# Fused attention and feed-forward on one core: the opening's order and all scheduling rules chosen anew

## Chip, cores, metric

The kernel runs on one core of a Trainium2 chip. The metric is the time of one execution on the device in microseconds (us), taken as the median of several runs. The profile gives a slightly shorter figure, the span from the first to the last instruction of one profiled execution (before: 703.6 us span, 705.5 us time).

## The reference

2048 tokens of width 640 are normalised. Attention with 32 heads of width 20, which share one key and one value head, and a feed-forward layer with squared ReLU both read the normalised tokens, and everything is summed.

```python
def reference(A_x, A_wq, A_wk, A_wv, A_wo, B_x, B_w1, B_b1, B_w2, B_b2):
    x = A_x                                   # 1 x 2048 x 640
    xn = _layernorm(x, axis=-1)
    # attention: q = xn @ wq (32 heads x 20), k = xn @ wk, v = xn @ wv (one head x 20)
    #   p = softmax(q k^T * 20 ** -0.5);  A = (p v, heads side by side) @ wo
    # feed-forward: h = relu(xn @ w1 + b1) ** 2;  B = h @ w2 + b2
    return x + A + B
```

## The kernel before

All 2048 score tiles (128 keys by 512 queries of one head) are made by TensorE and then need an exponential. ScalarE does most, two or three tiles in one instruction:

```python
return Op(f"ACT{st_['j']}", "ACT", 0.05 + 0.4267 * n, [lambda e: e.activation(
    out=PT[:, s0:s0 + n, :], in_=ps[:, b0:b0 + (n - 1) * db + 1:db, :],
    func=AF.Exp, bias=-EXP_SHIFT, scale=SCALE)], deps)
```

VectorE does the rest in *sets* of four tiles: it turns each score into the bit pattern of an exponential (with TensorE, GpSimd and more passes of VectorE behind it).

The program orders its own instructions while it is built: a list scheduler picks the next instruction of each engine by estimates, under some twenty numbers that may be set anew for each 10 us of the kernel's time, a *stage*:

```python
STG = 10.0
RULES = {3: {'PVA': 2.1, 'PVD': 2.1, 'R3': 1, 'PP': 0.9},
         ...                                   # cut: 49 more stages
         69: {'R3': 0, 'JIT': 1.1}}
PRIO = {'NM15': 2.12, 'NM10': 2.88, 'PW2': 0.96}          # hand-set order of single instructions
NBEF = {'AG4': 10.21, 'NM7': 11.5, 'Qe0_1': 10.11, 'PW12': 25.33}   # not before this time
QEACT = (0, 1, 2, 3)                           # query copies of the opening on ScalarE
ACTST = (2, 5, 6)                              # token tiles whose statistics ScalarE takes
POOLXN = (2, 7, 9, 10, 11, 13, 14, 15)         # token tiles that GpSimd normalises
```

The opening loads 16 token tiles of 128 tokens. Each needs statistics, a normalisation (`XN`), a transpose on TensorE (`T`) and a copy of that (`TE`). Four token tiles make a *key group*: one key product, one copy of it, and then 4 x 4 heads = 16 score tiles of the first query block become possible. Once the attention begins, ScalarE is to have scores without a break.

The softmax here doesn't subtract the row's maximum and nothing guards it: scores larger than these inputs give would overflow.

## Time and profile before

| before | |
|---|---|
| time, median of 3 runs | 705.52 us (704.88 to 706.26) |
| first exponential starts | 15.30 us |
| ScalarE idle between exponentials in the opening | 0.39 us at 28.15, 2.35 us at 32.44 |
| exponentials | 715 instructions, 1480 tiles |
| VectorE score tiles | 568 (142 sets) |
| last exponential ends | 695.14 us |
| from there to the end (tail) | 8.50 us |

The table is read from ScalarE's timeline and the page's groups; the prediction shows those lines of the timeline and the chain. In the page's groups, below, the columns are: line, engine, operation, output and input, count, then busy time and mean ns, then idle time just before and what ended it. These two rows of the kernel before split the score tiles between ScalarE and VectorE:

```profile
L910 ACT ACTIVATE PT<-ps 128x1024 bf16<-128x1024 f32 (+1 forms) x715 | 677.1, 1219 | 3.8 <-PE ps L367 3.8
L1083 DVE TENSOR_SCALAR tmore<-ps 128x512 uint16<-128x512 f32 x568 | 367.4, 683 | 31.7 <-PE ps L367 28.2
```

ScalarE waited only 3.8 us in all for scores, so it is the bound.

### The profile page before, as it was taken

To read this page: it belongs to the slowest core of one execution; us is meant where nothing else is said; L and a number is where in the kernel's file an instruction comes from. 1 tells how busy PE (TensorE), PEld (TensorE's weight loads), DVE (VectorE), ACT (ScalarE), POOL (GpSimd) and SP (SyncE) were. 2 spreads that over 40 slices of the span, in tenths; PEclk is the share of its full clock that TensorE was granted. 3 is DMA by queue.
4 is the path that set the end of the run, shared out by engine and by line. 5 is a ranking of instruction groups with operands and counts; after the bars stand their busy time and mean duration, and the time that the engine had idled before them with its cause. 6 is when DMAs were issued, how large, how long until landed. Compare 5 with 4: busy or idle time off the path is not lost.

```text
span 703.6 us, 22608 instructions
## 1 busy us (share of the span) xinstructions
PE 695.0 (99%) x9780; PEld 216.0 (31%) x9781; DVE 645.9 (92%) x1125; ACT 687.5 (98%) x739; POOL 427.3 (61%) x268
## 2 busy tenths in 40 slices
PE   8999999999999999999999999999999999999997
PEld 4422223233322223332322222323333222233333
DVE  7789999999999998989998998899899999999894
ACT  6899999999999999999999999999999999999995
POOL 4767556567566764666568765766665675644253
PEclk9999999999999999999999999999999999999999
DMA  6325422233337701211101001111112100031201
GB/s 201 98 70 153 115 78 58 81 97 80 84 85 160 162 20 25 55 40 37 52 18 40 23 22 28 29 47 26 46 42 51 36 22 23 20 106 51 55 26 39
DMA packets 42016, 44.00 MB, mean 63 GB/s; under 512 B 15540, under 2 KB 32772, under 8 KB 41788
## 3 DMA queue, kind: packets, MB, share of 16 engines
q1 hardware_dynamic: 39132, 36.93, 19.2%
q0 software_dynamic: 2208, 5.25, 3.9%
q8 instruction: 76, 1.25, 0.7%
q10 hardware_dynamic: 576, 0.38, 0.2%
q14 instruction: 24, 0.20, 0.1%
HBM read 28.03 MB, written 14.91 MB: 61 GB/s over the span
## 4 chain that ended last, share of the span: by engine, by line
ACT 95%; PE 4%; DMA 1%; DVE 0%; SPq 0%; issue 0%; DVEq 0%
ACT PT L910 94%; PE ps L367 3%; DMA x_sb<-in_A_x_dram 1%; PE ps L540 1%; ACT xnT L477 0%; ACT OC L421 0%; DVE out_sb L1164 0%; PE ps L568 0%; SPq L384 0%; ACT OC L422 0%; SPq L391 0%; PE ps L510 0%; PE ps L496 0%; DVEq L227 0%; DVE PT L1164 0%
## 5 line engine op out<-in xcount | busy, mean ns | idle before, releaser
L910 ACT ACTIVATE PT<-ps 128x1024 bf16<-128x1024 f32 (+1 forms) x715 | 677.1, 1219 | 3.8 <-PE ps L367 3.8
L1083 DVE TENSOR_SCALAR tmore<-ps 128x512 uint16<-128x512 f32 x568 | 367.4, 683 | 31.7 <-PE ps L367 28.2
L1101 POOL TENSOR_SCALAR tmore<-tmore 128x2048 uint16<-128x2048 uint16 x109 | 206.4, 1900 | 171.1 <-PE ps L367 62.3
L367 PE MATMUL ps<-qT,kT 20*128 20x512 bf16 x2048 | 281.7, 384 | 1.9 <-ACT PT L910 0.8
L1101 POOL TENSOR_SCALAR x_sb<-tmore 128x2048 uint16<-128x2048 uint16 x100 | 189.3, 1902 | 79.4 <-DVE x_sb L1101 24.2
L367 PEld LDWEIGHTS ps<-qT,kT 20*128 20x128 bf16 x2048 | 71.6, 91 | 280.4 <-ACT PT L910 233.1
L367 PE MATMUL ps<-PT,vx 128*32 128x512 bf16 x1480 | 136.9, 386 | 0.2 <-ACT PT L910 0.2
L1101 DVE TENSOR_SCALAR x_sb<-tmore 128x2048 uint16<-128x2048 uint16 x135 | 96.1, 745 | 0.1
L367 PE MATMUL ps<-x_sb,vxs 128*32 128x512 bf16 x940 | 83.2, 382 | 0.0
L367 PE MATMUL ps<-xnT,w_sb 128*32 128x512 bf16 x960 | 77.2, 384 | 0.1
L367 PE MATMUL ps<-w_sb,big 128*32 128x320 bf16 x1536 | 74.5, 302 | 0.0
L367 PE MATMUL ps<-tmore,vxs 128*32 128x512 bf16 x764 | 69.6, 382 | 0.0
L1101 DVE TENSOR_SCALAR tmore<-tmore 128x2048 uint16<-128x2048 uint16 x82 | 61.5, 770 | 0.1
L367 PE MATMUL ps<-tmore,vx 128*32 128x512 bf16 x568 | 55.7, 382 | 0.0
L367 PEld LDWEIGHTS ps<-PT,vx 128*32 128x32 bf16 x1480 | 34.9, 94 | 62.1 <-issue 53.6
L367 PEld LDWEIGHTS ps<-w_sb,big 128*32 128x32 bf16 x1536 | 32.1, 95 | 29.3 <-issue 22.2
L648 DVE TENSOR_SCALAR hT_tmp<-ps,b1col 128x512 bf16<-128x512 f32 x48 | 35.8, 746 | 3.4 <-PE ps L367 2.7
L367 PE MATMUL ps<-xnT,wq_sb 128*32 128x512 bf16 (+1 forms) x480 | 33.7, 356 | 0.2 <-DVE tmore L1083 0.2
L367 PE MATMUL ps<-wo_c,OC 128*32 128x320 bf16 x608 | 30.9, 301 | 0.0
L367 PEld LDWEIGHTS ps<-x_sb,vxs 128*32 128x32 bf16 x940 | 21.3, 95 | 19.9 <-issue 13.4
L367 PEld LDWEIGHTS ps<-xnT,w_sb 128*32 128x32 bf16 x960 | 17.6, 94 | 26.7 <-issue 22.4
L367 PEld LDWEIGHTS ps<-tmore,vxs 128*32 128x32 bf16 x764 | 18.1, 95 | 16.4 <-issue 11.5
(81 smaller groups left out, 259.4 us busy)
## 6 DMA issues: line engine op xcount, KB each, us to landing
xbd<-b2d SPq DMA_DIRECT2D x16, 320.0 KB, 4.4
xbd<-in_A_x_dram POOLq DMA_DIRECT2D x8, 640.0 KB, 5.8
xr<-xbd SPq DMA_DIRECT2D x32, 160.0 KB, 2.4
w_sb<-in_B_w_dram SPq DMA_DIRECT2D x8, 480.0 KB, 4.4
big<-OR SPq DMA_DIRECT2D x71, 40.0 KB
big<-drs SPq DMA_DIRECT2D x71, 40.0 KB
out_dram<-out_sb SPq DMA_DIRECT2D x15, 160.0 KB, 1.8
qT<-QCr SPq DMA_DIRECT2D x108, 20.0 KB
```

The source lines that it names most:

```text
L367: return lambda e: e.matmul(out_, l, r, start=start, stop=stop, tile_position=tp)
L540: return [(lambda e, dt=dt: e.transpose(out=psbf(bk)[:, dt * 128:(dt + 1) * 128], in_=xn_sb[:, st, dt:D:DT], identity=ident[:])) for dt in ...
L648: o = Op(f"RL{qc}_{f}", "DVE", 0.66, [lambda e: e.tensor_scalar(out=hT_tmp[:, k % 2, :], in0=ps[:, bk, :], scalar1=b1col[:, f:f + 1], scal ...
L910: return Op(f"ACT{st_['j']}", "ACT", 0.05 + 0.4267 * n, [lambda e: e.activation(out=PT[:, s0:s0 + n, :], in_=ps[:, b0:b0 + (n - 1) * db + ...
L1083: d1 = op(f"D1_{n}_{i}", "DVE", 0.60, lambda e: e.tensor_scalar(out=L[:, cs].bitcast(U16), in0=ps[:, bank, :], scalar1=XA, scalar2=XB, op0 ...
L1101: p = op(f"P{j}_{n}", eng, 0.60 if eng == "DVE" else 1.86, lambda e, T=T, j=j, two=two: e.tensor_scalar(out=T.bitcast(U16), in0=L.bitcast( ...
```

## The change

The intent is a quicker opening (ScalarE does fewer query copies and its statistics earlier, some hand-set delays go), a gate that keeps VectorE from taking a score while it is busy, and new rules for every stage. Cut to its core:

```diff
-RULES = {3: {'PVA': 2.1, 'PVD': 2.1, 'R3': 1, 'PP': 0.9},
-         ... (cut: 50 more stages)
+DJIT = 9.0
+RULES = {2: {'DRATE': 1.1, 'DGAP': 1.5, 'JIT': 1.1},
+         ... (cut: 52 more stages; 'DJIT': 0.3 in stages 67 to 69 alone)
-PRIO = {'NM15': 2.12, 'NM10': 2.88, 'PW2': 0.96}
-NBEF = {'AG4': 10.21, 'NM7': 11.5, 'Qe0_1': 10.11, 'PW12': 25.33}
+PRIO = {'XN1': 0.13}
+NBEF = {'S4a': 6.0, 'AG5': 10.23, 'PW1': 4.94}
-QEACT = (0, 1, 2, 3)
+QEACT = (0, 1)
-FFN0 = 0.3
+FFN0 = 0.6
-ACTST = (2, 5, 6)
-POOLXN = (2, 7, 9, 10, 11, 13, 14, 15)
+ACTST = (0, 2, 4)
+POOLXN = (7, 9, 10, 11, 13, 14, 15)
@@ make_dqk: a score tile for VectorE
+            if max(free["DVE"], free["PE"]) + sum(o.dur for o in dve_q if o.frees is not None) > free["PE"] + 0.43 + par("DJIT"):
+                return None
```

More of the change, by code (lines that the diff above doesn't have):

```diff
@@ L80 @@
 KEEP = 1
-RULES = {3: {'PVA': 2.1, 'PVD': 2.1, 'R3': 1, 'PP': 0.9},
-         4: {'PVA': 2.1, 'PVD': 2.1, 'R3': 1, 'PP': 0.9, 'WARM': 0.78},
-         5: {'D1P': 1, 'MPRIO': 0.5, 'PBIAS': 2.5},
-         6: {'D1P': 1, 'MPRIO': 0.5, 'PBIAS': 2.5, 'ND': 1, 'QKP': 0},
-         7: {'DQP': 2.05, 'URG': 2, 'PVD': 2.1, 'BEHIND': -0.3},
-         8: {'WARM': 0.85, 'DQP': 0.95},
-         10: {'ND': 1, 'NOPEN': 3},
-         11: {'ND': 1, 'NOPEN': 3},
-         12: {'EPS': 0.12},
-         13: {'EPS': 0.06, 'EVP': 0.3},
-         15: {'PBIAS': 0},
-         17: {'EPS': 0.06},
-         18: {'EPS': 0.12},
-         19: {'WARM': 0.78, 'PBIAS': 2.5, 'IDLE': 0.3},
-         21: {'PBIAS': 0, 'KEEP': 0},
-         23: {'EPS': 0.12},
-         25: {'R3': 1, 'EVP': 0.3},
-         26: {'R3': 1, 'EVP': 0.3, 'IDLE': 0.3, 'PVD': 2.1},
-         28: {'EPS': 0.12, 'URG': 3},
-         29: {'EPS': 0.12, 'URG': 3, 'KEEP': 3, 'EVP': 1.1, 'ND': 3},
-         31: {'PBIAS': 1, 'D1P': 1, 'PVD': 1.05},
-         32: {'PBIAS': 1, 'D1P': 1, 'PVD': 1.05, 'DGAP': 0.8, 'DQP': 0.95, 'SQP': 2, 'R3': 1},
-         36: {'PP': 0.9, 'BEHIND': -0.1, 'EVP': 0.3, 'PBIAS': 1.5},
-         37: {'URG': 3, 'JIT': 1.0, 'PVD': 1},
-         38: {'SQP': 0.7, 'URG': 3},
-         39: {'PP': 2.5},
-         40: {'PBIAS': 1},
-         41: {'PBIAS': 1, 'DGAP': 1.5, 'SQP': 0.7},
-         42: {'PBIAS': 1, 'DGAP': 1.5, 'SQP': 2, 'NOPEN': 3, 'ND': 2, 'PVD': 1},
-         43: {'PBIAS': 1, 'DGAP': 1.5, 'SQP': 2, 'NOPEN': 3, 'ND': 2, 'PVD': 1, 'R3': 9},
-         44: {'WARM': 0.78, 'KEEP': 3, 'DLAST': 7.5},
-         45: {'DGAP': 0.8, 'KEEP': 1, 'D1P': 3},
-         48: {'PBIAS': 1},
-         49: {'PBIAS': 1, 'R3': 1},
-         50: {'PBIAS': 1, 'R3': 1},
-         53: {'DLAST': 3.5},
-         54: {'DLAST': 3.5, 'EPS': 0, 'EVP': 0.3},
-         55: {'DLAST': 3.5, 'EPS': 0, 'EVP': 0.3, 'ND': 1},
-         56: {'EVP': 2, 'MPRIO': 1.0},
-         57: {'R3': 1, 'ND': 1},
-         58: {'BEHIND': -0.1, 'EPS': 0, 'PP': 4, 'R3': 1},
-         59: {'BEHIND': -0.1, 'EPS': 0, 'PP': 4, 'R3': 1, 'DRATE': 0.95, 'DLAST': 10, 'PVA': 2.1},
-         60: {'EVP': 1.1},
-         61: {'EVP': 1.1, 'SQP': 0.7},
-         62: {'EVP': 1.1, 'SQP': 0.7, 'KEEP': 3, 'R3': 1, 'NOPEN': 2, 'D1P': 3},
-         64: {'PP': 0.9, 'DRATE': 0.8},
-         65: {'R3': 1},
-         66: {'R3': 1},
-         67: {'EPS': 0.12, 'PVA': 1.05},
-         68: {'R3': 0},
-         69: {'R3': 0, 'JIT': 1.1}}
@@ new lines @@
+DJIT = 9.0
+RULES = {2: {'DRATE': 1.1, 'DGAP': 1.5, 'JIT': 1.1},
+         3: {'D1P': 0.5, 'R3': 1, 'IDLE': 0.2},
+         4: {'D1P': 0.5, 'R3': 1, 'IDLE': 0.2, 'JIT': 0.75, 'DGAP': 1.5, 'WARM': 0.72},
+         6: {'PBIAS': 1},
+         7: {'D1P': 3, 'DLAST': 8.5},
+         8: {'D1P': 3, 'DLAST': 3.5, 'DQP': 0.95, 'ND': 1, 'PVD': 0.95},
+         9: {'D1P': 3, 'DLAST': 3.5, 'DQP': 0.95, 'ND': 1, 'PVD': 0.95},
+         10: {'D1P': 3, 'DLAST': 3.5, 'DQP': 0.95, 'ND': 1, 'PVD': 0.95, 'URG': 2, 'PP': 2.5},
+         11: {'DQP': 3, 'PBIAS': 2.5, 'MPRIO': 0.9},
+         12: {'DQP': 3, 'PBIAS': 2.5, 'MPRIO': 0.9, 'PP': 2.5},
+         13: {'DQP': 3, 'PBIAS': 2.5, 'MPRIO': 0.9, 'PP': 2.5},
+         14: {'DQP': 3, 'PBIAS': 2.5, 'MPRIO': 0.9, 'PP': 2.5, 'D1P': 3},
+         15: {'DQP': 3, 'PBIAS': 2.5, 'MPRIO': 1.1, 'PP': 2.5, 'D1P': 3, 'NOPEN': 3},
+         16: {'DQP': 3, 'PBIAS': 2.5, 'MPRIO': 1.1, 'PP': 2.5, 'D1P': 3, 'NOPEN': 3, 'EPS': 0.06},
+         17: {'DQP': 3, 'PBIAS': 2.5, 'MPRIO': 1.1, 'PP': 2.5, 'D1P': 3, 'NOPEN': 3, 'EPS': 0.06},
+         18: {'D1P': 1, 'DRATE': 0.8, 'PBIAS': 1.5},
+         19: {'D1P': 1, 'DRATE': 0.8, 'PBIAS': 1.5},
+         20: {'ND': 2, 'R3': 9, 'EPS': 0.06},
+         24: {'NOPEN': 1},
+         25: {'IDLE': 0.5, 'PBIAS': 2.5},
+         26: {'IDLE': 0.5, 'PBIAS': 2.5, 'SQP': 0.7, 'PP': 2.5},
+         27: {'IDLE': 0.5, 'PBIAS': 2.5, 'SQP': 0.7, 'PP': 2.5, 'URG': 6, 'BEHIND': 0.12},
+         28: {'IDLE': 0.5, 'PBIAS': 2.5, 'SQP': 0.7, 'PP': 2.5, 'URG': 6, 'BEHIND': 0.05, 'NOPEN': 1, 'D1P': 3},
+         29: {'IDLE': 0.5, 'PBIAS': 2.5, 'SQP': 0.7, 'PP': 2.5, 'URG': 6, 'BEHIND': 0.05, 'NOPEN': 1, 'D1P': 3},
+         33: {'DQP': 2.05, 'QKP': 0, 'KEEP': 3},
+         34: {'DQP': 2.05, 'QKP': 0, 'KEEP': 3, 'PP': 0.9},
+         35: {'KEEP': 3},
+         36: {'KEEP': 3, 'DRATE': 1.1, 'DQP': 0.95},
+         37: {'JIT': 0.75, 'MPRIO': 0.9, 'PP': 0.9, 'PVD': 1.05},
+         43: {'DRATE': 0.95, 'WARM': 0.85, 'PBIAS': 1.5},
+         44: {'R3': 0, 'JIT': 0.9, 'DQP': 2.05},
+         45: {'R3': 0, 'JIT': 0.9, 'DQP': 2.05},
+         46: {'DLAST': 3.5, 'D1P': 0.5, 'R3': 1},
+         47: {'DLAST': 3.5, 'D1P': 0.5, 'R3': 1, 'EPS': 0, 'QKP': 0},
+         48: {'DLAST': 3.5, 'D1P': 0.5, 'R3': 1, 'EPS': 0, 'QKP': 0, 'DGAP': 0, 'PP': 0.9},
+         49: {'DLAST': 3.5, 'D1P': 0.5, 'R3': 1, 'EPS': 0, 'QKP': 0, 'DGAP': 0, 'PP': 0.9, 'PBIAS': 0},
+         50: {'PP': 0.9, 'PBIAS': 1.5},
+         51: {'DLAST': 4.5},
+         52: {'PVA': 1, 'PBIAS': 0.3},
+         53: {'PVA': 1, 'PBIAS': 0.3, 'R3': 1, 'IDLE': 2, 'WARM': 0.78},
+         56: {'PBIAS': 1.5, 'DQP': 3, 'DGAP': 0.8, 'JIT': 1.0},
+         57: {'R3': 2, 'URG': 6, 'PP': 2.5},
+         58: {'R3': 2, 'URG': 6, 'PP': 2.5, 'DQP': 0.95, 'IDLE': 2, 'D1P': 0.5},
+         59: {'WARM': 0.78, 'EVP': 2},
+         60: {'PVA': 1, 'R3': 1},
+         61: {'R3': 2, 'KEEP': 3},
+         63: {'DQP': 2.05, 'R3': 1, 'D1P': 0.5, 'NOPEN': 2},
+         64: {'DQP': 2.05, 'R3': 1, 'D1P': 0.5, 'NOPEN': 2, 'URG': 2, 'PVA': 1, 'PBIAS': 0},
+         65: {'DQP': 2.05, 'R3': 1, 'D1P': 0.5, 'NOPEN': 2, 'URG': 2, 'PVA': 1, 'PBIAS': 0},
+         66: {'DQP': 2.05, 'R3': 1, 'D1P': 0.5, 'NOPEN': 2, 'URG': 6, 'PVA': 1, 'PBIAS': 0, 'PP': 0.9, 'DRATE': 0.95},
+         67: {'DQP': 2.05, 'R3': 1, 'D1P': 0.5, 'NOPEN': 2, 'URG': 6, 'PVA': 1, 'PBIAS': 0, 'PP': 0.9, 'DRATE': 0.95, 'DJIT': 0.3, 'JIT': 0.82},
+         68: {'DQP': 2.05, 'R3': 0, 'D1P': 0.5, 'NOPEN': 2, 'URG': 6, 'PVA': 1, 'PBIAS': 0, 'PP': 0.9, 'DRATE': 0.95, 'DJIT': 0.3, 'JIT': 0.82},
+         69: {'DQP': 2.05, 'R3': 0, 'D1P': 0.5, 'NOPEN': 2, 'URG': 6, 'PVA': 1, 'PBIAS': 0, 'PP': 0.9, 'DRATE': 0.95, 'DJIT': 0.3, 'JIT': 1.0, 'EPS': 0.12}}
@@ L159 @@
 DEFAULTS = dict(EVP=EVP, PBIAS=PBIAS, MPRIO=MPRIO, DGAP=DGAP, DLAST=DLAST, DRATE=DRATE, BEHIND=BEHIND, IDLE=IDLE, URG=URG, NOPEN=NOPEN,
-                EPS=0.03, JIT=JIT, R3=R3, STATIC=STATIC, PVA=1, PVD=1, D1P=1, PP=4, SQP=2, DQP=3, QKP=0, ND=2, WARM=WARM, KEEP=KEEP)
+                EPS=0.03, JIT=JIT, R3=R3, STATIC=STATIC, PVA=1, PVD=1, D1P=1, PP=4, SQP=2, DQP=3, QKP=0, ND=2, WARM=WARM, KEEP=KEEP, DJIT=DJIT)
 class Ctr:
```

## The prediction

> **What bounds the kernel now.** I read the page first (busy shares, then the chain that ended last), then the chain in order of time, then ScalarE's timeline, then the order of the instructions in both built programs. The page:
>
> ```profile
> PE 695.0 (99%) x9780; PEld 216.0 (31%) x9781; DVE 645.9 (92%) x1125; ACT 687.5 (98%) x739; POOL 427.3 (61%) x268
> ...
> ACT 95%; PE 4%; DMA 1%; DVE 0%; SPq 0%; issue 0%; DVEq 0%
> ```
>
> TensorE and ScalarE both look full, so the busy shares decide nothing; the chain does: 95% of the span is ScalarE, the exponentials (line 910). The chain in order of time says where it is not ScalarE:
>
> ```profile
> 14.94 0.32 PE ps L367 x2
> ...
> 28.42 0.41 PE ps L540 x5
> 28.83 2.06 PE ps L367 x36
> 30.89 0.59 PE ps L568 x20
> 31.48 0.59 PE ps L540 x10
> 32.07 0.35 PE ps L367 x3
> 32.42 0.02 issue
> 32.44 661.79 ACT PT L910 x699
> 694.23 0.04 issue
> 694.27 3.90 PE ps L367 x104
> ```
>
> So there are three stages: an opening to 32.44 us, 662 us in which ScalarE never stops, and a tail from the last exponential (it ends at 695.14) to 703.64, 8.5 us. ScalarE's timeline shows what the opening costs:
>
> ```profile
> 13.69 0.56 ACT L493 ACTIVATE qT<-ps 128x128 bf16<-128x128 f32 x2
> 15.30 12.46 ACT L910 ACTIVATE PT<-ps 128x1024 bf16<-128x1024 f32 x13 [1.05 <-PE ps L367]
> 28.15 1.94 ACT L910 ACTIVATE PT<-ps 128x1024 bf16<-128x1024 f32 x2 [0.39 <-PE ps L367]
> 32.44 28.46 ACT L910 ACTIVATE PT<-ps 128x1536 bf16<-128x1536 f32 x30 [2.35 <-PE ps L367]
> ```
>
> The first exponential starts at 15.30; 15 of them (31 score tiles, one instruction being of three tiles) run before 32.44, and ScalarE idles 0.39 + 2.35 us. The 31 are no accident: keys of token tiles 0 to 7 give 8 x 4 heads = 32 tiles, and the 32nd goes in one instruction with two tiles of the third key group. The timelines of the other engines show why that group is late:
>
> ```profile
> 26.67 0.14 DVE L432 TENSOR_SCALAR mv<-mv 128x1 f32<-128x1 f32 x1
> ...
> 28.87 0.49 DVE L543 COPY xnT<-ps 128x640 bf16<-128x640 bf16 x1 [0.27 <-PE ps L540]
> 30.94 0.75 DVE L554 TENSOR_SCALAR kT<-ps,nk 128x512 bf16<-128x512 f32 x1 [1.58 <-PE ps L367]
> ```
>
> ```profile
> 26.91 0.88 POOL L436 TENSOR_SCALAR big<-x_sb,mv,rstd 128x640 bf16<-128x640 bf16 x1 [0.23 <-DVE mv L432]
> ```
>
> By the program's order the row at 26.67 negates the mean of token tile 10. It was held back on purpose (an entry of the old PRIO table), and GpSimd's normalisation of tile 10, its transpose (28.35), its copy (28.87), the third key product (29.63 to 30.88), the key copy (30.94 to 31.69) and the scores (32.00) follow one upon the other.
>
> **What the Trainium skill says.** (1) "Perfetto Trace Analysis", Identifying the Most-Contended Engine: matmul busy share is no good measure of TensorE's headroom. The trace agrees: beside 99% busy, weight loads wait 238.9 us in 602 waits for the exponentials. (2) "ScalarE: Activation LUTs", What ACT_TABLE_LOAD costs: 0.833 ns per element plus a fixed part. The trace agrees on the slope: from start to start the median is 904 ns after a two-tile exponential and 1330 ns after a three-tile one, so 426 ns per 512-column tile and 52 ns per instruction. The fixed part is smaller than the page's numbers would leave after its stated overlap (280 - 93 = 187 ns); I use 52. (3) "SBUF — State Buffer", Who interferes with whom: VectorE and GpSimd share a port pair that one of them locks. The normalisation takes 0.44 us on VectorE and 0.88 on GpSimd, and the kernel orders the two; no row isolates a collision.
>
> **The change part by part.** The short description says ScalarE takes tiles 2 and 4 only; the diff has (0, 2, 4), and the built program has three pairs of statistics on ScalarE, as before.
>
> *Work on ScalarE.* Counted in the built order: exponentials of two tiles 665 to 656, of three 50 to 57, of one 0 to 1. That is 1480 to 1484 tiles in 715 to 714 instructions; VectorE scores 568 to 564. So one set of four tiles moves to the bound engine: 4 x 0.426 - 0.052 = +1.65 us. The gate on VectorE scores has DJIT = 9.0 by default, 0.3 only in stages 67 to 69 (the last 30 us), so it can bite only near the end; this set is the likely effect.
>
> *First exponential.* Before, after x tile 4 landed at 7.85, ScalarE did a statistic, two transposed copies, a statistic, a q copy, two statistics, and so on to 14.25. After, one statistic pair (tile 4), four transposed copies and two q copies follow: the pair of tile 6 (0.83 + 0.81) and two q copies (2 x 0.28) leave, 2.2 us. But the path moves to VectorE: tiles 0 and 2 are normalised only after VectorE has waited for x tile 4 (7.88) and done four half-tile statistics (0.40 each): 9.13 and 9.49. Transpose 0 then stands behind K1: 9.63; ScalarE is busy to 10.59 as before, copies at 10.59 and 11.2; K0, Q0, V0 and Q2, V2 on TensorE at about 0.88 a group to 13.0; two warm fills, K2, K3 (0.28 each): first scores at 14.0, first exponential 0.43 later (as 14.87 to 15.30 before): **14.4**, 0.9 earlier.
>
> *Second key group.* Tile 7's copy ends about 18.5, the product needs its last chunk after a score whose bank the sixth exponential frees (start 14.4 + 5 x 0.904 = 18.9, +1.14 as before = 20.1): key copy 20.9 to 21.65; V, two transposes and one chunk on TensorE stand before the next scores: 22.2, exponential at 22.65 against 21.65 at which ScalarE would be free. A **new gap of 1.0** where before had none.
>
> *Third key group.* The held-back entry is gone: tile 10's mean is at 22.7 on VectorE, its GpSimd normalisation at 24.0, tile 11's at 24.8, copies at 26.3 and 26.7, key product 27.2 to 28.9 (a score waits inside it), key copy 28.95 to 29.7, scores 29.85, exponential **30.3**. ScalarE could go on at 29.35: gap about 1.0. The number of tiles done before it is again 31, so this restart compares directly with 32.44: 2.1 us earlier. All these are estimates from the durations of the trace of before.
>
> *Middle.* Starts are late by 8.4 us in sum against 904 and 1330 (gaps left out), nearly all in steps where TensorE had 0.9 us or more of other work between two scores. Such steps number 179 before and 184 after; weighting each class by its mean lateness gives the same sum within 0.1 us. The new rules are a reshuffle: 0, give or take 1.5.
>
> *Tail.* After the last transpose TensorE has 16 chunks left instead of 14 (+0.28 us), but the end is set by VectorE's row of six output sums (698.69 on): 0 to +0.1.
>
> Sum: -2.1 + 1.65 + 0 + 0.05 = **-0.4 us**. Lean another 0.3 for the reason that rules "chosen anew" were chosen for something: 705.5 - 0.7 = **704.8 us**.
>
> **Rivals.** (A) The reshuffled rules hit TensorE's slack worse: more warm fills (7 against 3 in the attention, 25 against 20 full-width ones in the opening) and scores waiting for two VectorE evictions (25 against 16) speak for it; then lateness grows by 1 to 2 us: 706.5. (B) The rules cut the lateness, as that is what a scheduler would search for; up to half of 8.4 is there: 701.5. For it speaks only intent; the count of long steps speaks against it. (C) The opening gains nothing, since a gap at the second key group grows as the one at the third shrinks: the restart is then near 32 and the extra set is left as a loss, 706.7. Against it: the held-back entry is a clear 4 us of slack that was thrown away.
>
> **Range and chances.** The opening is good to about 0.8 us, the middle 1.5, run to run 0.7: together about 1.9. So 8 in 10 within **703.0 to 706.6**. A change of 2% is 14 us, more than all lateness, gaps and opening idle together: faster by over 2% 0.01, within 0.98, slower 0.01.
>
> **What would show it.** Right: 714 exponentials busy about 678 to 679 us; first one near 14.4; a gap near 21.7 and one before about 30.3; the key copy of the third group near 29; weight loads still waiting over 200 us for exponentials; a tail of 8.4 to 8.7 us. Wrong: an exponential stage after the restart that is not 664.5 us (662.7 + 1.7) within 1.5, or a restart outside 29.5 to 31.2. A fresh gap in the middle, or near 37 us where the fourth key group is due, would sink the number.

## More of the kernel before

A new set is opened only when many conditions hold, among them that the block's queries and keys are there:

```python
def new_set():
    ...                                        # cut: how much of the block is left
    if b >= NBLK or not (b == 0 or b in qt_op):
        return None
    ok = [kt for kt in unclaimed[b] if kt_ok(kt) and kt // 4 in vs_op]
    if not ok:
        return None
    n = len(sets)
    if 3 not in kt_op:                         # the fourth key group must have been issued
        return None
    ...                                        # cut: buffers free
```

## The result, and the profile after

The changed kernel took **707.58 us** (median of 4, 707.12 to 707.70) against 705.81 us (median of 4) of the kernel before in the same rounds. The ratio is 1.0026, 95% interval 1.0008 to 1.0043. A ratio here is the mean time of one kernel's fast runs over that of the other's of the same rounds, so it is not quite the ratio of the two medians. So it is 1.8 us slower and above the range of the prediction.

The page of the profile after: busy shares, chain by engine, and the same two groups as above.

```profile
PE 696.9 (99%) x9790; PEld 217.5 (31%) x9790; DVE 641.9 (91%) x1121; ACT 689.2 (98%) x736; POOL 426.2 (60%) x267
...
ACT 94%; PE 5%; DVE 1%; DMA 0%; POOL 0%; issue 0%; DVEq 0%
...
L913 ACT ACTIVATE PT<-ps 128x1024 bf16<-128x1024 f32 (+1 forms) x714 | 679.3, 1222 | 4.7 <-PE ps L370 4.5
L1088 DVE TENSOR_SCALAR tmore<-ps 128x512 uint16<-128x512 f32 x564 | 364.9, 681 | 37.2 <-PE ps L370 33.9
```

The bound is the same. ScalarE is busy 2.2 us longer with exponentials: VectorE did 564 tiles, 4 fewer, and they are now ScalarE's (1.65 of the 2.2 us by the prediction's sum). Its idle time before exponentials grew by 0.9 us. ScalarE's timeline of the opening, after (start, length, engine, line, operation, count, and in brackets the idle time before):

```profile
14.55 7.44 ACT L913 ACTIVATE PT<-ps 128x1024 bf16<-128x1024 f32 x8 [1.97 <-PE ps L370]
22.90 7.13 ACT L913 ACTIVATE PT<-ps 128x1024 bf16<-128x1024 f32 x6 [0.91 <-PE ps L370]
30.68 7.74 ACT L913 ACTIVATE PT<-ps 128x1536 bf16<-128x1536 f32 x7 [0.66 <-PE ps L370]
39.41 4.20 ACT L913 ACTIVATE PT<-ps 128x1536 bf16<-128x1536 f32 x4 [0.98 <-PE ps L370]
```

The first three rows are what the prediction expected, 14.4, 22.65 and 30.3. The fourth is not: ScalarE stops again at 38.4 us, where before it ran through. To see what each gap is worth, I compared the two traces not at equal times but at equal work: when does ScalarE begin the exponential that follows N finished tiles? (Where N differs by one between them, the tile is counted as 0.452 us, half of a two-tile exponential.)

| tiles done on ScalarE | before starts the next at | after | after is ahead by |
|---|---|---|---|
| 0 | 15.30 | 14.55 | 0.75 |
| 17 / 16 | 23.07 | 22.90 | -0.28 |
| 31 (third key group) | 32.44 | 30.68 | **1.76** |
| 47 (fourth key group) | 39.67 | 39.41 | **0.26** |
| 100 to 1400 | | | -0.04 to 0.45 |

So 1.5 of the 1.76 us that the third key group won were given back at the fourth, 9 us later. The chain of waits of the changed kernel, in order of time, shows what stood before it:

```profile
27.60 2.12 PE ps L370 x31
29.72 0.59 PE ps L571 x20
30.32 1.95 PE ps L370 x25
32.26 0.41 PE ps L543 x5
...
34.38 0.41 PE ps L543 x5
34.78 0.32 PE ps L370 x2
35.10 0.41 PE ps L543 x5
35.51 2.49 PE ps L370 x33
38.00 0.60 PE ps L571 x20
38.59 0.11 PE ps L589
38.70 0.68 PE ps L370 x7
39.41 6.96 ACT PT L913 x7
```

L543 is a transpose of a token tile, L370 products (from 35.51 the fourth key product with scores between), L571 values. From 27.60 to 39.38 the chain is TensorE's own work, one piece after another. The four transposes of the fourth group start at 32.26, 33.32, 34.38 and 35.10; GpSimd had normalised the last of these tiles by 33.46:

```profile
31.74 1.72 POOL L439 TENSOR_SCALAR big<-x_sb,mv,rstd 128x640 bf16<-128x640 bf16 x2
```

So the last two transposes, at least, waited for their turn on TensorE and not for their data (the scheduler, which orders by its estimates, may have placed them so because it expected the tiles later). The key product comes late, and all that follows with it. VectorE's timelines show two consequences. First the kernel before, then the changed one (key copy of the fourth group, then VectorE's first score tiles):

```profile
35.13 0.75 DVE L554 TENSOR_SCALAR kT<-ps,nk 128x512 bf16<-128x512 f32 x1 [1.80 <-PE ps L367]
...
36.88 2.53 DVE L1083 TENSOR_SCALAR tmore<-ps 128x512 uint16<-128x512 f32 x4
```

```profile
37.84 0.75 DVE L557 TENSOR_SCALAR kT<-ps,nk 128x512 bf16<-128x512 f32 x1 [1.80 <-PE ps L370]
...
41.63 1.29 DVE L1088 TENSOR_SCALAR tmore<-ps 128x512 uint16<-128x512 f32 x2 [0.56 <-PE ps L370]
```

The fourth key copy is 2.7 us later, and VectorE takes its first score tile 4.75 us later. At 568 tiles in some 652 us (36.9 to 689) VectorE does 0.87 tiles a microsecond, so 4.75 us are about 4 tiles: one set. Counting VectorE's score tiles begun by a given time, the changed kernel is behind by 5 at 40 us, 3 at 100 us, 2 at 310 us, 4 at 500 us, 3 at 630 us and 4 at the end. This suggested that the set was lost at the start (theory A below).

The last surprise is in the tail, 9.11 us instead of 8.50. VectorE's last sum ends 6.03 us after the last exponential in both kernels; what differs is SyncE. Its timeline at the end, before and then after:

```profile
699.98 1.30 SPq L708 DMA_DIRECT2D out_dram<-out_sb  x3
701.33 0.45 SPq L708 DMA_DIRECT2D out_dram<-PT  x1
```

```profile
701.45 1.90 SPq L711 DMA_DIRECT2D out_dram<-out_sb  x3
703.39 0.46 SPq L711 DMA_DIRECT2D out_dram<-PT  x1
```

Three output transfers take 1.90 us to issue instead of 1.30: the second alone took 0.99 instead of 0.38, and the rest follows it.

### The profile page after: what moved, and what is told of

Read it like the earlier page. It is cut to its first block, busy times and chain, and to the rows that moved or that the text cites. A ratio compares the mean times of both kernels' runs of the same rounds, so it can differ in the third digit from the quotient of the medians.

```text
span 705.7 us, 22611 instructions
## 1 busy us (share of the span) xinstructions
PE 696.9 (99%) x9790; PEld 217.5 (31%) x9790; DVE 641.9 (91%) x1121; ACT 689.2 (98%) x736; POOL 426.2 (60%) x267
## 4 chain that ended last, share of the span: by engine, by line
ACT 94%; PE 5%; DVE 1%; DMA 0%; POOL 0%; issue 0%; DVEq 0%
ACT PT L913 94%; PE ps L370 3%; DMA x_sb<-in_A_x_dram 0%; PE ps L543 0%; PE ps L571 0%; PE ps L513 0%; DVE out_sb L1169 0%; PE ps L478 0%; DVE xnT L546 0%; PE ps L499 0%; DVE OR L429 0%; DVE OR L430 0%; POOL rstd L437 0%; DVE big L439 0%; DVE mv L431 0%
## 5 line engine op out<-in xcount | busy, mean ns | idle before, releaser
L370 PE MATMUL ps<-qT,kT 20*128 20x512 bf16 x2048 | 281.5, 384 | 2.5 <-ACT PT L913 1.1
L1106 POOL TENSOR_SCALAR x_sb<-tmore 128x2048 uint16<-128x2048 uint16 x110 | 208.4, 1908 | 109.5 <-PE ps L370 32.7
L1106 POOL TENSOR_SCALAR tmore<-tmore 128x2048 uint16<-128x2048 uint16 x99 | 187.5, 1906 | 138.9 <-PE ps L370 41.8
L370 PEld LDWEIGHTS ps<-qT,kT 20*128 20x128 bf16 x2048 | 71.7, 91 | 277.6 <-ACT PT L913 228.3
L370 PE MATMUL ps<-PT,vx 128*32 128x512 bf16 x1484 | 137.9, 386 | 0.3
L1106 DVE TENSOR_SCALAR x_sb<-tmore 128x2048 uint16<-128x2048 uint16 x125 | 88.9, 740 | 0.0
L370 PE MATMUL ps<-x_sb,vxs 128*32 128x512 bf16 x940 | 84.4, 383 | 0.0
L370 PE MATMUL ps<-xnT,w_sb 128*32 128x512 bf16 x960 | 76.4, 383 | 0.0
L370 PE MATMUL ps<-w_sb,big 128*32 128x320 bf16 x1536 | 75.6, 302 | 0.0
L370 PE MATMUL ps<-tmore,vxs 128*32 128x512 bf16 x752 | 68.5, 382 | 0.0
L1106 DVE TENSOR_SCALAR tmore<-tmore 128x2048 uint16<-128x2048 uint16 x89 | 67.0, 772 | 0.1
L370 PE MATMUL ps<-tmore,vx 128*32 128x512 bf16 x564 | 55.4, 383 | 0.0
L370 PEld LDWEIGHTS ps<-PT,vx 128*32 128x32 bf16 x1484 | 35.3, 94 | 64.2 <-issue 53.7
L370 PEld LDWEIGHTS ps<-w_sb,big 128*32 128x32 bf16 x1536 | 32.3, 95 | 29.0 <-issue 21.8
L370 PE MATMUL ps<-xnT,wq_sb 128*32 128x512 bf16 (+1 forms) x480 | 33.4, 356 | 0.0
L370 PE MATMUL ps<-wo_c,OC 128*32 128x320 bf16 x608 | 31.7, 301 | 0.0
L370 PEld LDWEIGHTS ps<-x_sb,vxs 128*32 128x32 bf16 x940 | 22.2, 95 | 21.4 <-issue 15.3
L370 PEld LDWEIGHTS ps<-xnT,w_sb 128*32 128x32 bf16 x960 | 18.5, 94 | 27.1 <-issue 21.5
L659 DVE TENSOR_TENSOR big<-hT_tmp 128x512 bf16<-128x512 bf16 x48 | 22.6, 486 | 0.0
```

Of the source, the lines that this page charges most:

```text
L370: return lambda e: e.matmul(out_, l, r, start=start, stop=stop, tile_position=tp)
L659: q = op(f"SQ{qc}_{f}", "DVE", 0.34, lambda e: e.tensor_tensor(out=h2T[:, f, :], in0=hT_tmp[:, k % 2, :], in1=hT_tmp[:, k % 2, :], op=ALU. ...
L1106: p = op(f"P{j}_{n}", eng, 0.60 if eng == "DVE" else 1.86, lambda e, T=T, j=j, two=two: e.tensor_scalar(out=T.bitcast(U16), in0=L.bitcast( ...
```

## The experiments

Three questions: what is one set worth, and why was it lost (A: by VectorE's late start; B: by the gate or the late rules; C: it is worth nothing and the loss is elsewhere; these letters are not those of the prediction's rivals)? What did the fourth key group wait for? And what is wrong in the tail?

### after_again: the changed kernel once more

No edit; run beside the kernel before on the same chip as the next three.

> The changed kernel unaltered, beside the kernel before on the same chip: 1.5 to 2.1 us slower. If the 0.6 us in the tail (one output transfer whose issue took 0.99 us on SyncE in the first profile) is chance, the tail of this profile is 8.5 us again and the difference is nearer 1.5; if it belongs to the new order, it is 9.1 us again.

707.60 us (5 runs) against 705.71 (9 runs): ratio 1.0027, interval 1.0014 to 1.0040. The tail was 9.22 us, so it isn't chance. From 47 tiles on, the two traces of the changed kernel keep the same distance to within 0.02 us. But this execution began its exponentials at 14.85, not 14.55, and here it was 0.04 us *behind* the kernel before at 47 tiles and 0.12 us ahead at 1400. The reason is chance in the loading: in the profiled runs the load of token tiles 4 and 5 landed anywhere from 6.98 to 8.02 us (7.85 in the trace of before, 7.31 in the first of after, 8.01 here). Of the five profiles of the changed opening, the two in which it landed at 8.0 start at 14.84 and 14.85, the three in which it landed at 7.14 to 7.46 start at 14.55 to 14.61. The 0.26 us of the first pair lie within this scatter: at 47 tiles the two profiles of the opening of before (before and before_141) stand at 39.67 and 39.36, mean 39.51, the five of the changed one (after, after_again, gate_off, rules_142, rules_142_fetch) at 39.41 to 39.71, mean 39.54. **The opening is worth nothing beyond the fourth key group.**

### before_141: one set fewer, nothing else

```diff
             n = len(sets)
+            if n >= 141:
+                return None
```

> The kernel before with VectorE's score sets capped at 141, so that only the last set moves to ScalarE; opening unchanged. Theory A (a set of four tiles on ScalarE costs what its exponentials cost: 4 x 0.426 - 0.052 us): +1.65 us over before, 0 difference in the opening, 715 exponential instructions. Rival C (the lost set is hidden in slack and the loss lies elsewhere): less than +0.5 us.

707.05 us against 705.71: +1.3 us, ratio 1.0020 (1.0007 to 1.0032). The profile resolves it better: from the first exponential's start to the last one's end the kernel before took 679.84 us and this one 681.53, **+1.69 us**. The row of VectorE's scores and that of the exponentials:

```profile
L910 ACT ACTIVATE PT<-ps 128x1024 bf16<-128x1024 f32 (+1 forms) x715 | 678.8, 1223 | 3.8 <-PE ps L367 3.8
L1085 DVE TENSOR_SCALAR tmore<-ps 128x512 uint16<-128x512 f32 x564 | 364.3, 682 | 33.6 <-PE ps L367 30.1
```

1.7 us more busy, the idle time the same. C falls: a set costs its exponentials in full.

### gate_off: without the gate

```diff
-         67: {..., 'DJIT': 0.3, 'JIT': 0.82},
+         67: {..., 'JIT': 0.82},
          (and the same in 68 and 69)
```

> The changed kernel with the gate on VectorE scores removed from stages 67 to 69. Theory A (the set was lost at the start, not at the end): still 564 VectorE score tiles (141 sets), the time within 0.4 us of the changed kernel. Rival B (the gate turned a set away): 568 tiles and about 1.65 us less than the changed kernel.

708.11 us, ratio to before 1.0033 (1.0019 to 1.0046). Still 564 tiles on VectorE: the gate did not turn the set away. It was even 0.5 us slower than the changed kernel (expected: within 0.4); its tail was 9.84 us, 0.6 longer, so the tail theory had to explain that too.

### old_open_new_rules and new_open_old_rules: the halves exchanged

The first is the changed kernel with the opening settings of before (ACTST, POOLXN, QEACT, PRIO, NBEF, FFN0), the second the reverse.

> The changed kernel with all the opening settings of the kernel before (which tiles ScalarE takes statistics of, which GpSimd normalises, who copies queries, the hand-set order entries), new rules kept. The built program has 134 VectorE sets, 8 fewer than before. If a rule list is good only for the opening that it was chosen on: 8 x 1.65 = 13 us for the sets alone, so about 719 us or more. If the opening and the rules are independent: about 706.

> The kernel before with all opening settings of the changed kernel and its own rules kept. The built program has 137 VectorE sets, 5 fewer than before. If rules and opening belong together: 5 x 1.65 = 8 us for the sets and some more for gaps, 714 us or more. If they are independent: about 705.

723.12 us (2 runs, ratio 1.0247) and 719.95 us (2 runs, ratio 1.0187). The sets account for 8 x 1.65 = 13.2 and 5 x 1.65 = 8.3 us; new waits in the middle, up to 1.4 us each in the first and one of 3.6 us at 596 us in the second, for most of the rest. Each of the two rule lists fits only the opening that it was chosen for, so the halves of this change can't be valued by exchanging them, and neither run tells what the opening alone is worth.

### fetch_shift: TensorE's instruction fetches moved

Among the DMA queues of the trace there is one, queue 8, that carries instructions in packets of 16 KB: 76 packets before, 77 after. The Trainium skill, "Runtime: NRT & Kernel Launch", Instruction fetch mechanics, says that an engine's instructions are refilled in blocks of 16 KiB, 256 instructions, over a DMA queue of its own. The trace agrees: 76 packets of 16 KB for the 9780 + 9781 rows of TensorE are 64 bytes each, so queue 8 is TensorE's. In four traces (after, after_again, gate_off, before_141) the second output transfer's issue ended 0.38 us after such a fetch that had begun shortly before it. To test it I moved the fetches, by more instructions in the opening's warm-up products:

```diff
-            return [lambda e: e.matmul(ps[:, PVB, :], ones_bf[:, :], hT_tmp[:, 0, :], start=True, stop=True)]
+            return [lambda e, c=c: e.matmul(ps[:, PVB, c:c + 128], ones_bf[:, :], hT_tmp[:, 0, c:c + 128], start=True, stop=True)
+                    for c in range(0, 512, 128)]
```

> The changed kernel with each of the 25 full-width warm-up products of the opening split into four of 128 columns: 75 more product-and-load pairs on TensorE, 150 instructions, so that TensorE's instruction fetches (queue 8, 16 KB each) fall earlier against the tail; order and attention otherwise the same. Theory T (the tail of 9.1 us instead of 8.5 is the second output transfer waiting for a fetch that is in flight: its issue ended 0.39 us after the fetch in four traces): the last fetch moves from 4.8 us after the last exponential to about 2, the transfer's issue takes 0.38 us again, the tail is 8.5 us, and the kernel is 0.6 us faster than the changed one, about 707.0. Rival (the tail belongs to the new order of work, or to chance): tail 9.1 us, 707.6.

The fetch moved to 2.21 us and the tail was 8.53 us, as theory T says:

```profile
702.80 1.33 SPq L711 DMA_DIRECT2D out_dram<-out_sb  x3
704.18 0.45 SPq L711 DMA_DIRECT2D out_dram<-PT  x1
```

Yet the kernel was not clearly faster: 708.34 us against 706.57 of before on this chip, ratio 1.0023 (1.0009 to 1.0036). The changed kernel did not run on this chip; its own ratios are 1.0026 and 1.0027, with intervals that overlap this one. Its profile lost what it had gained: TensorE stood still for 0.17 us at 13.4 us, and from the first exponential to the last it took 682.81 instead of 682.07 us, 0.24 of it at one place (236 us) and the rest spread thinly, though the 714 exponentials are the same in number and size. Why that spread grew is left open.

### fourth_group: token tile 13 back on VectorE

```diff
-POOLXN = (7, 9, 10, 11, 13, 14, 15)
+POOLXN = (7, 9, 10, 11, 14, 15)
```

> The changed kernel with the normalisation of token tile 13 given back to VectorE, so that the fourth key group comes earlier. Theory (the fourth group's gap is a late GpSimd normalisation chain, tiles 13 to 15): the gap of 0.98 us at 39.4 us is gone, that at 30.7 us grows by 0.3 to 0.5 us, and by 100 tiles ScalarE is about 0.5 us ahead of the changed kernel. The whole is slower, for the rules were not chosen for this opening: the built program has 138 VectorE sets (3 fewer, 5 us). Rival (the fourth group is bound by TensorE's work before it): the gap stays at 1 us.

ScalarE's timeline of the opening:

```profile
22.95 7.13 ACT L913 ACTIVATE PT<-ps 128x1024 bf16<-128x1024 f32 x6 [0.91 <-PE ps L370]
31.29 12.18 ACT L913 ACTIVATE PT<-ps 128x1536 bf16<-128x1536 f32 x11 [1.21 <-PE ps L370]
```

The gap of the fourth group is gone and that of the third grew by 0.55 us (expected: 0.3 to 0.5); at 100 tiles ScalarE was 0.55 us *ahead* of the changed kernel (expected: about 0.5) though it had been 0.61 us behind at 31. The reason that I gave was wrong, however. The fourth key copy came at 37.72 instead of 37.84, just 0.12 us sooner: as the chain above shows, it is TensorE's row of work, and not the normalisation on GpSimd, that holds it, so for the key copy the rival was right. Taking the four transposes earlier on TensorE wasn't tried. What made the gap go is that one more tile of the earlier groups was done before ScalarE needed the fourth (48 instead of 47, 0.45 us), and that the 0.6 us by which the third group was later came out of the wait at the fourth. **A delay of 0.6 us at the third group cost nothing; the fourth set the restart.** The whole took 727.9 us (2 runs, ratio 1.030), for 138 sets and some fifteen new waits; I put them down to the rules, as in the exchanged halves.

### rules_142: the lost set brought back by late rules

The opening is identical. Six late stages differ from the changed kernel:

```diff
+         62: {'D1P': 0.5},
-         63: {..., 'R3': 1},
+         63: {...},
-         64: {..., 'PBIAS': 0},
+         64: {..., 'PBIAS': 0, 'ND': 3},
-         66: {..., 'PBIAS': 0, ...},
+         66: {..., 'PBIAS': 2.5, ...},
-         67: {..., 'PBIAS': 0, ..., 'DJIT': 0.3, 'JIT': 0.82},
+         67: {..., 'PBIAS': 2.5, ..., 'JIT': 0.82},
-         69: {..., 'EPS': 0.12}
+         69: {...}
```

> The changed kernel, opening identical, with the rules of six late stages (62 to 64, 66, 67, 69) altered so that the built program has 142 VectorE sets again. Theory A1 (the set was lost for good when VectorE's scores began 4.75 us late): the set can only be bought by idle time elsewhere, so ScalarE has at least 1 us of new gap near the end and the time is within 0.8 us of the changed kernel. Rival A2 (the set is a matter of the late rules alone, worth its 1.65 us): 1.2 us or more faster than the changed kernel with no new gap.

707.83 us against 706.57, ratio to before 1.0014 (1.0001 to 1.0026). The set is back (568 tiles): level with the changed kernel up to 630 us, four tiles ahead at 670. But ScalarE has a new wait:

```profile
669.07 14.84 ACT L914 ACTIVATE PT<-ps 128x1024 bf16<-128x1024 f32 x15
684.87 11.47 ACT L914 ACTIVATE PT<-ps 128x1024 bf16<-128x1024 f32 x11 [0.96 <-PE ps L371]
```

This start came 1.34 us later than two-tile exponentials in a row would. First to last exponential took 681.49 us, 0.58 less than in the changed kernel. So the strict form of theory A, that the set was lost for good, is wrong: late rules can restore it. (The gate alone was excluded by gate_off; the late rules were not.) But they paid 1.34 of its 1.65 us for it. The tail was 9.69 us, the longest but one.

### rules_142_fetch: the same once more

An unaltered repeat, in spite of its name.

> A repeat of the run with 142 sets, unaltered, for a second sample of its time on this chip: 0.6 to 1.0 us slower than before, tail 9.7 us, gap of 1.34 us at about 685 us.

707.36 us against 705.67, ratio 1.0022 (1.0009 to 1.0035), worse than the first sample by as much as such intervals allow; the two together put it some 1.3 us above before. The gap was 1.34 us again. The tail was 9.10, not 9.69 as expected: the fetch took 0.96 us instead of 1.41 this time.

### before_fetch: a fetch meant for the tail of the kernel before

```diff
+            w = 128 if free["PE"] < 6.0 else 512
-            return [... 512 columns ...]
+            return [... pieces of w columns ...]
```

> The kernel before with only its first nine warm-up products (all done by 6.3 us, in idle time) split into four pieces each: 54 more TensorE instructions, nothing else changed. Theory T (an instruction fetch in flight delays the second output transfer, its issue ending 0.38 us after the fetch): the last two fetches of queue 8, one of which was 0.75 us after the last exponential, fall near -0.2 and 4.7 us, the transfer's issue takes about 1 us instead of 0.38, the tail is 9.1 to 9.3 us instead of 8.50, and the kernel is 0.6 to 0.8 us slower than before. Rival (the late issue belongs to the order of work of the changed kernel): tail 8.50 us, no difference.

A miss: the fetch came at 4.07 us, not 4.7, and ended at 5.23. The transfer's issue then ended as before at 5.64, the tail was 8.51 us and the time 705.30 against 705.67 (ratio 0.9995). It does not show the slowdown that I wanted, but it fits the rule that the next table shows: 5.23 + 0.38 = 5.61 is just early enough.

### fetch_early and rules_142_early: the fetch moved, from the first nine products only

The same edit with `w = 64`, in the changed kernel and in rules_142.

> The changed kernel with only its first nine warm-up products split, into eight pieces each: 126 more TensorE instructions, all before 6.5 us, so that the opening isn't slowed as in the run that split all 25. Theory T: last fetch about 2.4 us after the last exponential, tail 8.5 us, 0.6 to 0.7 us faster than the changed kernel, so about 1.3 us slower than before. Rival: tail 9.1 us, 1.9 us slower than before.

> The kernel with 142 sets and, besides, the first nine warm-up products split into eight pieces each (126 more TensorE instructions before 6.5 us). Theory T: the last fetch moves from 5.05 us after the last exponential to about 2.6, the tail from 9.69 to 8.5 us, and the kernel is 1.1 us faster than without the split, within 0.5 us of the kernel before: of the loss of 1.9 us the set (less its gap) and the fetch are then the whole. Rival: no change.

Both tails shrank to 8.54 and 8.50 us. fetch_early: 707.46 us, ratio 1.0025 (1.0010 to 1.0040), a gain of at most a few tenths on the changed kernel, where 0.6 to 0.7 was expected. rules_142_early: 706.96 us, ratio 1.0016 (1.0003 to 1.0028), 0.4 us faster than its unsplit twin on the same chip, not 1.1 (the twin's own tail was 9.10 this time, so 0.6 was to be had). In the profiled runs the missing part lies in the opening, with a stop of TensorE at 13 us once more. Its timeline in rules_142_early:

```profile
12.71 0.29 PE L371 MATMUL ps<-xnT,wq_sb 128*20 128x128 bf16 x7
13.22 0.39 PE L371 MATMUL ps<-xnT,wq_sb 128*20 128x128 bf16 x13 [0.23 <-issue]
```

A product of 20 instructions is cut after the seventh, and the engine waits for nothing that the profile shows; the changed kernel ran all 20 in 0.46 us. The first exponential of this run started at 15.31, against 14.61 and 14.84 in the two runs of rules_142; the stop is 0.44 us of that (the product took 0.90 instead of 0.46). The splitting had moved the end of a fetched block here too; that this is the cause of the stop I only argue.

The tail of all profiled kernels, in us after the last exponential's end (read from the trace's packets and SyncE's issues; only fetches of queue 8 nearest the transfer):

| run | fetch in flight | second transfer's issue ends | tail |
|---|---|---|---|
| before | 0.75 to 1.63 | 5.64 | 8.50 |
| fetch_shift | 2.21 to 3.51 | 5.66 | 8.53 |
| old_open_new_rules | 1.13 to 2.12 | 5.70 | 8.57 |
| fourth_group | -1.17 to 0.13 | 5.66 | 8.53 |
| new_open_old_rules | 4.12 to 5.08 | 5.67 | 8.54 |
| before_fetch | 4.07 to 5.23 | 5.64 | 8.51 |
| before_141 | 4.32 to 5.40 | 5.78 | 8.65 |
| after | 4.77 to 5.86 | 6.25 | 9.11 |
| rules_142_fetch | 4.90 to 5.86 | 6.24 | 9.10 |
| after_again | 4.78 to 5.98 | 6.37 | 9.22 |
| rules_142 | 5.05 to 6.46 | 6.84 | 9.69 |
| gate_off | 5.14 to 6.61 | 6.99 | 9.84 |
| fetch_early | 2.31 to 3.70 | 5.66 | 8.54 |
| rules_142_early | 2.55 to 3.95 | 5.63 | 8.50 |

The issue ends at 5.64 or 0.38 us after the fetch, whichever is later, in every row to within 0.06 us. Where the fetch was moved away, the tail shrank each time. Another queue of instructions, 14, had a packet of 8 KB at 4.92 in the changed kernel too; it was still there at 4.93 in fetch_shift and 4.92 in fetch_early, where the tail was short, so it isn't the cause. This settles the tail: **a fetch of TensorE's instructions in flight delayed SyncE's output transfer**. It is not a rule for every transfer: in the trace of before, a load of queries at 555.67 has an issue of 1.65 us that ends 0.39 us after a fetch, but another at 537.71, with the usual 0.71 us, ends while a fetch is in flight. What decides it, and the cause inside the DMA engines, isn't shown.

## Why the prediction was wrong, point by point

**What bounds the kernel.** Right: ScalarE's exponentials, in both kernels.

**Work on ScalarE, +1.65 us.** Right, and shown: +1.69 us in before_141. Its guess that the gate was the likely effect was wrong: gate_off keeps 141 sets. What lost the set isn't settled. VectorE's start 4.75 us later is of the right size and the deficit is there from the start, though it falls to 2 tiles by 310 us; rules_142 shows that it can be made good late, at nearly its price.

**First exponential, 14.4.** Nearly right: 14.55. The gain over before was mis-sized, since both starts move by some tenths with the landing of a load. Over the five profiles with this unsplit opening the mean start is 14.68; before and before_141 give 15.30 and 14.99, so about 0.5 us and not 0.9.

**Second key group.** Right: a new gap, 0.91 us idle (predicted 1.0) at 22.90 (22.65).

**Third key group, "2.1 us earlier".** The restart was 30.68 against 30.3, so the time was mis-sized by 0.4, and ScalarE was ahead by 1.76 and not 2.1. But **this is the step that failed**: it took the restart at the third group for the worth of the whole opening ("this restart compares directly with 32.44: 2.1 us earlier") and entered -2.1 in the sum. The same comparison one group later, at 47 tiles, gives 0.26 us in that pair of traces and -0.04 in the next. The opening's entry should have been 0 (what its late VectorE start may have done to the set apart). The prediction named the symptom as a thing that "would sink the number", a gap where the fourth key group is due, and did not work it out. Its test of the stage after the restart (664.5 us within 1.5) did not catch it: it took 665.9 us, just inside.

**Middle, 0.** Right. From 47 tiles to the end of the last exponential both kernels have 693 instructions to go. Before took 655.47 us for them, the changed kernel 657.21 in both of its traces: 1.74 us more, of which its four tiles more are 4 x 0.426 = 1.70. (The 0.2 us that it seems to gain by 1400 tiles come from counting tiles: by then it has done more of them by threes.)

**Tail, 0 to +0.1.** Wrong by size: +0.6 and +0.7 us. TensorE's longer end was hidden, as it said (VectorE's last sum ends 6.03 us after the last exponential in both); what it lacked was a fetch under the output transfers.

**Lean, -0.3.** It was a guess from intent and not a mechanism; no run bears it out.

With what was measured for after_again against the first trace of before, the sum is 0.04 (opening, to 47 tiles) + 1.74 (from there to the last exponential: the set) + 0.72 (tail) = +2.5 us, the difference of the two spans, 706.1 and 703.6. The medians are only 1.9 us apart; this execution of the changed kernel was the slowest of its five. Rival C of the prediction (706.7) came nearest, with an opening that gains nothing; but it expected the loss at the second group and a restart near 32, and the restart was at 30.68 and the loss at the fourth. No version beat the kernel before: the best with the new opening, rules_142_early, remains 1.1 to 1.3 us above it (rules_142 had a ratio of 1.0014 in its first sample and 1.0022 in its second).

## What to carry to other kernels

When work arrives in groups, take an opening's worth at the *last* group that the bound engine waits for, and compare at equal work done, not at one restart: gains before it are only slack for the next wait. Here a tuned rule list belonged to the exact order that it was tuned on (three runs with another opening were 13 to 21 us slower than before), so parts of such a change can't be judged by swapping them; cap or move one thing while all else stands. And a difference of half a microsecond in an unchanged tail may be nothing in the program but where the instruction stream is refilled.

## What the Trainium skill lacked or had wrong

- "Runtime: NRT & Kernel Launch", Instruction fetch mechanics, calls the cost of crossing a 16 KiB boundary "mostly hidden", which speaks of the engine that fetches. Here it wasn't hidden for another engine: a TensorE fetch of about 1 us in flight kept SyncE's output transfer back until 0.38 us after its end, 0.6 to 1.3 us of tail in five profiled runs. No page names an instruction fetch as the cause of another engine's late transfer.
- "ScalarE: Activation LUTs", What ACT_TABLE_LOAD costs: the fixed part of an exponential in a row of them. Less its stated overlap, the page's numbers leave 187 ns with a pointer operand, or 93 ns with immediates (estimates from its figures); from start to start the traces show 904 ns for 1024 columns, 52 ns beyond the 426 ns per 512 columns. The slope agrees.
- No page says how much a first load's landing scatters from run to run: here from 6.98 to 8.02 us with the same issue order at the start, which moves the first exponential by some 0.3 us and hides differences of that size between single profiles of the opening.
